# Hash attention and a gated feed-forward layer in one kernel: another order of the opening, and the second head pair hashed as one

## The chip, the core and the metric

The kernel runs on one core of a Trainium2 chip. The core has five engines that each work through their own list of instructions in order and wait for each other by semaphores: TensorE (PE; its weight loads are shown as PEld), VectorE (DVE), ScalarE (ACT), GpSimd (POOL) and SyncE (SP). [...] Loads and stores between memory and SBUF are DMAs, issued by SP and GpSimd (and one or two by ScalarE). The metric is device time in microseconds (us), the median of the runs.

## The reference

Inputs are q, k, v of shape (4, 8, 768, 64), that is 4 batches and 8 heads, a projection of 64 x 6, and the weights of a gated feed-forward layer (512 wide, 1536 inside).

```python
q_bits = (np.einsum('bhsd,dk->bhsk', q, proj) > 0)      # 6 bits a token, k the same
q_bucket = np.sum(q_bits * 2 ** np.arange(6), axis=-1)  # k_bucket the same
mask = q_bucket[:, :, :, None] == k_bucket[:, :, None, :]
scores = np.where(mask, (q @ k.T) / 8, -1e9)
attn = softmax(scores)                                  # + 1e-9 in the divisor
x = (attn @ v) as (4 * 768 tokens, 512)
xn = x / sqrt(mean(x * x) + 1e-6) * rms_g
out = (silu(xn @ w_gate) * (xn @ w_val)) @ w_out
```

A query sees only the keys whose six hash bits are the same as its own.

## The kernel before

**The mask as extra rows of a product.** Scores come from one product per 128 keys and 384 queries. Its operands lie in a buffer QK: rows 0 to 63 hold k or q in fp16, rows 64 to 75 twelve rows of hash bits (six bits and their complements, scaled by -32 and 16), so that a key and a query with different bits get a large negative score. A score product reads 76 rows (`KROWS`) or, for the pairs listed in `score_rows`, all 128; rows 76 to 127 must then be zero, which `clear_rows` writes. There are six QK buffers, `qkbuf`, taken in turn by (batch, head pair): pairs (0,0) to (0,3) get 0 to 3, (1,0) and (1,1) get 4 and 5, (1,2) gets 0 again.

**How k, q and bits get there.** A load brings raw rows. For batch 0 and the first two pairs of batch 1, `keep` turns a head's k or q on TensorE (three 128 x 128 products with the identity, tile t_ps) and copies it from PSUM to an fp32 tile (kT, qT); `cast_half` casts 64 rows at a time to fp16 into QK, on GpSimd, and for one half of q on ScalarE. `hash_bank` multiplies the fp32 tiles with the projection, four products into one PSUM bank (d_ps), `signs` compares on VectorE and writes the tile bits, and twelve-row pieces of it are moved into QK by VectorE, GpSimd or a DMA. `hash_head` hashes one head per bank, `hash_heads` the two heads of a pair in one bank. In the kernel before, heads 0 to 3 of batch 0 are hashed one by one and the later pairs as pairs.

**Windows, turns, slots.** The work is cut into 8 windows w of 384 queries (two for each batch). A turn (w, hp) is one head pair of one window. `TURNS` gives their order: (0,0), (1,0), (0,1), (0,2), (0,3), (1,1), (1,2), (1,3), and so on. Each turn has two heads, each head three slots p of two key blocks. Slot g is one `scores` (two products into one of two PSUM tiles s_ps) and one `probs` (exp on ScalarE, 128 x 768). After a head's three slots, `av` multiplies the probabilities with v into the bank o_ps, in two halves. There is one o_ps bank; a turn's two heads fill it. `attn_out` then empties it on VectorE: an add (otmp) and a reciprocal (rcp). `attn_x` makes x and its squares sq, on GpSimd for most turns (for turns (0,2) and (0,3) on VectorE), and `sumsq` sums the squares on VectorE (ssp). When all four pairs of a window are done, `norm`, `scale_x` and `turn_x` make the layer's input, and `gate`, `value` and `project` are the feed-forward products of that window, spread between the score products of later slots.

**The order is written out by hand.** A dictionary `plan` holds what is emitted at each step s; the last loop goes through the steps: `scores(s + 1)`, then work of rank below 3, then `probs(s + 1)`, then the rest by rank. The order of emission is the order on each engine; nothing reorders it afterwards. So an operation that waits holds up everything that was planned after it on its engine. Window 0's gate products begin at step 42.

Three places in the plan matter here. The x of turn (0,1) and its squares come at step 20 (`o_step`), the emptying of o_ps for turn (0,2) at step 26, and the first AV product of turn (0,3), head 6, at step 28. Turns (0,0) and (1,0) end at steps 8 and 14; before, their x and squares come at steps 8 and 17 (`o_step`, `o_last`). The sums of squares of the turns (0,0), (1,0) and (0,1) come at steps 12, 18 and 24. Twice, GpSimd also issues halves of the weights, at steps 2 and 6 and at steps 19 and 24.

```python
at(end - 1, av, w, h, 0, 9)
at(end, av, w, h, 9, 18)
...
at(end, o_step, w, h // 2, rank=4.5)      # add, reciprocal, x, squares
...
at(end + late, s_step, w, h // 2, rank=5)  # sum of squares
```

Of the kernel before, what the change touches and what calls it, by code (L numbers as in the profile page):

```python
# [8 lines left out]
FP32 = mybir.dt.float32  # L9
# [7 lines left out]
S = 768  # L17
D = 64
# [3 lines left out]
HALF = 384  # L22
KROWS = D + 12
# [25 lines left out]
def kernel(  # L49
# [12 lines left out]
    nc = tc.nc  # L62
    PSUM = bass.MemoryType.PSUM

    const = ctx.enter_context(tc.tile_pool(name="const", bufs=1))
# [17 lines left out]
    pk = const.tile([128, 48], FP32, name="pk")  # L83
    pq = const.tile([128, 48], FP32, name="pq")
    thr = const.tile([128, 1], FP32, name="thr")
    scl = const.tile([128, 1], FP32, name="scl")
    mhalf = const.tile([128, 3], FP32, name="mhalf")
    gcol = const.tile([128, 4], FP32, name="gcol")
# [46 lines left out]
        if (b, hp) not in QK:  # L135
            QK[b, hp] = qkbuf[len(QK) % len(qkbuf)]

    def clear_rows(i):
        nc.gpsimd.memset(qkbuf[i][D:128].rearrange("p h n -> p (h n)").bitcast(FP32), 0.0)

    def score_rows(b, hp):
        return slice(0, 128 if (b, hp) in ((1, 0), (1, 1)) or b > 1 else KROWS)

    def t_tile(b, hp, which):
        T0[b, hp, which] = tpool.tile(
# [3 lines left out]
    def t0(b, h, which):  # L149
        hp, hh = divmod(h, 2)  # L150
        return T0[b, hp, which][:, hh * HALF : (hh + 1) * HALF]
# [35 lines left out]
    def keep(eng, b, h, which, room=None):  # L187
        ps = turn_pe(b, h, which, room)
        (eng.copy if eng is nc.scalar else eng.tensor_copy)(t0(b, h, which), ps)
# [155 lines left out]
    def idle(ps, n):  # L345

        for _ in range(n):
            nc.tensor.matmul(ps, ones16, ones16, start=True, stop=True)  # L348

    def scores(g):  # L350
        w, h, p = SLOTS[g]
        ps = scps.tile([128, 2, 512], FP32, name="s_ps")
        idle(ps[:, 0, HALF:512], {0: 8, 3: 6}.get(g, 0))
        for j in range(2):
            nc.tensor.matmul(  # L355
                ps[:, j, 0:HALF], k_cols(w // 2, h, 2 * p + j), q_cols(w, h),
                start=True, stop=True,
            )
        sps[g] = ps
# [25 lines left out]
    def attn_out(w, hp):  # L385
        b = w // 2
        if w not in x:
            x[w] = xpool.tile([128, 3, DMODEL], FP32, name="x")
            ssp[w] = xpool.tile([128, 3, 4], FP32, name="ssp")
        o = ot.pop((w, hp))  # L390
        tmp = spool.tile([128, 3, 2, 66], FP32, name="otmp")
        nc.vector.tensor_add(  # L392
            tmp[:, :, :, 0:65], o[:, :, :, 0:65],
            cvb[b % 2][:, 2 * hp : 2 * hp + 2, 0:65].unsqueeze(1).to_broadcast([128, 3, 2, 65]),
        )
        r = spool.tile([128, 3, 2, 1], FP32, name="rcp")
        nc.vector.reciprocal(r, tmp[:, :, :, 64:65])  # L397
        return tmp, r

    def attn_x(w, hp, tmp, r):  # L400
        xd = x[w][:, :, 128 * hp : 128 * hp + 128]
        urgent = (w, hp) in ((0, 2), (0, 3))
        eng = nc.vector if urgent else nc.gpsimd
        eng.tensor_mul(  # L404
            xd.rearrange("p c (h d) -> p c h d", h=2), tmp[:, :, :, 0:64],
            r.to_broadcast([128, 3, 2, 64]),
        )
        sq = spool.tile([128, 3, 128], FP32, name="sq")
        if urgent:
            for c in range(3):  # L410
                nc.vector.scalar_tensor_tensor(
                    out=sq[:, c], in0=xd[:, c], scalar=1.0, in1=xd[:, c],
                    op0=ALU.mult, op1=ALU.mult, accum_out=ssp[w][:, c, hp : hp + 1],
                )
        else:
            nc.gpsimd.tensor_mul(sq, xd, xd)  # L416
        return sq
# [97 lines left out]
        load_rows(nc.sync, 0, hp, which)  # L515

    nc.vector.memset(ones16, 1.0)
    make_identity(nc, ident)
    nc.gpsimd.dma_start(out=pn[64:128], in_=proj)
    nc.vector.memset(pm, 0.0)  # L520
# [21 lines left out]
    for i in range(2):  # L542
        nc.gpsimd.memset(vls[i][:, :, :, 64:65], 1.0)
        nc.gpsimd.memset(vsum[i][:, :, 64:65], 6.0)
    clear_rows(4)
    clear_rows(5)

    def load_w(dst, src, n0, n1):
        nc.gpsimd.dma_start(
# [15 lines left out]
    def columns_of_proj():  # L565
        rows = pn.unsqueeze(1).to_broadcast([128, 4, 6])
        for t, sign in ((pk, 1.0), (pq, -1.0)):
            nc.vector.scalar_tensor_tensor(
                out=t[:, 0:24].rearrange("p (c n) -> p c n", n=6), in0=pm, scalar=sign,
                in1=rows, op0=ALU.mult, op1=ALU.mult,  # L570
            )
# [5 lines left out]
    def casts(b, hp, i):  # L577
        for par in range(2):
            if not i % 2 or par:
                cast_half(b, 2 * hp + i // 2, "kq"[i % 2], par)  # L580
# [2 lines left out]
    keep(nc.scalar, 0, 0, "q")  # L583
    cast_half(0, 0, "q", 0, nc.scalar)
    columns_of_proj()
    idle(wz[:, 0:128], 5)
    bits0 = hash_head(0)
    keep(nc.scalar, 0, 1, "k")
    bits0((nc.vector, nc.vector, nc.vector))
    keep(nc.scalar, 0, 1, "q", scps.tile([128, 2, 512], FP32, name="s_ps")[:, 0, 0:HALF])  # L590
    casts(0, 0, 0)
    casts(0, 0, 2)
    cast_half(0, 1, "q", 0)
    scores(0)
    bits1 = hash_head(1)
    scores(1)
    probs(0)
# [9 lines left out]
    def at(s, f, *a, rank=3):  # L607
        plan[s].append((rank, len(plan[s]), lambda: f(*a)))
# [3 lines left out]

    moves = {}

    def hash_one(h):
        moves[h] = hash_head(h)
        moves[h]((nc.sync,), 3)

    def hash_pair(b, hp):
        moves[b, hp] = hash_heads(b, hp)  # L620
        odd = [(0, 2), (1, 2), (0, 3), (1, 3)]
# [2 lines left out]

    for h in range(2):
        at(1 + h, cast_half, 0, h, "q", 1)
        at(h, (bits0, bits1)[h], (nc.vector,), 3)

    for hp, turns, sv in ((1, (1, 2, 3, 5), 8), (2, (7, 8, 9, 10), 17), (3, (12, 13, 14, 15), 22)):
        for i, s in enumerate(turns):  # L630
            at(s, keep_pair, 0, hp, i)
            at(s + 1, casts, 0, hp, i)
            if i % 2:
                at(s + 2, cast_half, 0, 2 * hp + i // 2, "q", 0, nc.scalar)
        at(sv, v_prep, 0, hp)

    for h, s in ((2, 4), (3, 7)):
        at(s, hash_one, h)
        for t in range(3):
            at(s + 1 + t, lambda h=h, t=t: moves[h]((nc.vector,), t), rank=5)  # L640
    for hp, s, slots in ((2, 12, (13, 14, 15, 16)), (3, 17, (18, 19, 20, 21))):
        at(s, hash_pair, 0, hp)
        for i, s in enumerate(slots):
            at(s, lambda hp=hp, i=i: moves[0, hp](nc.vector, [divmod(i, 2)]), rank=5)
# [8 lines left out]


    for hp, loads, turns, sh, evens, sv in (
        (0, (9, 11, 13), (20, 21, 24, 27), 33, (41, 42), (27, 44)),
        (1, (13, 14, 36), (29, 31, 33, 35), 40, (45, 47), (49, 51)),
    ):
        for which, sl in zip("kqv", loads):
            at(sl, load_rows, nc.sync, 1, hp, which)  # L660
        for i, sl in enumerate(turns):
            at(sl, keep_pair, 1, hp, i)
            at(sl + 1, casts, 1, hp, i)
        at(sh, hash_pair, 1, hp)
        for hh, sl in enumerate(evens):
            at(sl, cast_half, 1, 2 * hp + hh, "q", 0)
        at(sv[0], v_prep, 1, hp)
        at(sv[1], v_sum, 1, hp)
# [30 lines left out]
    for hp, s in enumerate((48, 62, 64, 78)):  # L699
        at(s, v_mean, 1, hp, 2)  # L700

    for i, s in ((2, 76), (3, 78), (0, 97), (1, 98)):
        at(s, clear_rows, i, rank=6)

    gts, sqs = {}, {}
# [20 lines left out]
    for w in range(8):  # L726
        for h in range(H):
            end = LAST[w, h] + (2 if (w, h) == (0, 7) else 3)
            at(end - 1, av, w, h, 0, 9)
            at(end, av, w, h, 9, 18)  # L730
            if h % 2:
                if (w, h) == (1, 1):
                    at(end, o_first, w, 0, rank=4.5)
                    at(end + 3, o_last, w, 0, rank=4.5)
                else:
                    at(end, o_step, w, h // 2, rank=4.5)
                if (w, h) not in ((0, 5), (0, 7)):
                    late = 3 if h == 7 and w < 7 else 4
                    at(end + late, s_step, w, h // 2, rank=5)
        s0 = 24 * w + 42  # L740
        n0 = {0: 11, 2: 7, 3: 13, 4: 13, 5: 13, 6: 13}.get(w, 11)
        at(s0 - n0, norm, w, rank=5)
        for c in range(3):
            scale, rank = {0: 6, 2: 6 - c}.get(w, 8 - c), 1
            turn = {0: (4, 3, 2), 2: (4, 2, 1)}.get(w, (5, 3, 1))[c]
            if w in BY_DMA and c < 2:
                scale, turn, rank = 11 - c, 11 - c, 6
            at(s0 - scale, scale_x, w, c, rank=5)
            at(s0 - turn, turn_x, w, c, rank=rank)
        seen = set()  # L750
        for ft in range(NF):
            for f, s in ((g_step, s0 + 16 * ft // NF), (v_step, s0 + (32 * ft + 16) // (2 * NF))):
                at(s, f, w, ft, rank=4 if s in seen else 2)
                seen.add(s)
        for i in range(9 if w < 7 else 6):
            c, j = divmod(i, 3)
            at(s0 + 16 + i, project, w, c, 4 * j, 4 * j + 4, rank=1 if i == 8 else 3)
# [55 lines left out]
```

## Time and profile before

| | |
|---|---|
| median of 3 runs | 329.44 us (329.18 to 329.79) |
| the profiled execution | 329.47 us, of which the span of its instructions is 327.6 us |
| busy share of the span | TensorE 98%, VectorE 72%, ScalarE 64%, GpSimd 50% |
| first score product | 8.37 us |
| score products of slots 19 and 20 | 28.04 us |
| x of turn (0,1) on GpSimd | 32.53 us |
| first gate product | 48.72 us |

A row of a timeline gives start, duration, engine, line, operation, output<-input with shapes, and how often it ran in a row (x3 with one duration is the three together); the square bracket at its end is the idle time of the engine before it and what ended that. The chain of waits follows the end of the execution back to the start: at each step to what released it. A product's busy time includes its passage through the array, so that products in a row overlap: 0.48 us is shown for two score products of which the next can start 0.33 us later. GpSimd's spans are rough.

### The profile page before, as it was taken

What the parts mean: (1) busy time and instruction counts of PE and PEld (TensorE: products, weight loads), DVE (VectorE), ACT (ScalarE), POOL (GpSimd) and SP (SyncE); (2) the same over time, 40 slices, a digit from 0 to 9 for tenths busy, and PEclk for the clock granted to TensorE, in tenths of its full rate; (3) what the DMA queues carried; (4) which work ended last, traced back from release to release, by engine and by line L of the source; (5) the groups of instructions that cost most, each with busy time, mean ns of one, the idle gap of its engine ahead of it and who ended that gap; (6) DMA issues with size and microseconds to landing.
All of it is one profiled execution on the core that took longest, in us unless ns stands there. A gap on an engine that the chain in (4) does not pass through costs nothing.

```text
span 327.6 us, 7853 instructions
## 1 busy us (share of the span) xinstructions
PE 321.5 (98%) x2975; PEld 199.5 (61%) x2975; DVE 234.9 (72%) x526; ACT 208.1 (64%) x324; POOL 165.4 (50%) x238
## 2 busy tenths in 40 slices
PE   8998999999999999999999999999999999999995
PEld 7576766655566556655566656566566656655654
DVE  4798896888598976989487865967267824793860
ACT  3788986775576666657576766667677766423331
POOL 7887977278658685686734274733221320230000
PEclk9999999999999999999999999999999999999999
DMA  7998988984359729911470814001200012002002
GB/s 216 358 212 244 165 131 154 151 179 70 119 109 172 128 48 226 155 39 26 130 128 18 150 24 152 3 18 22 78 32 2 11 24 98 0 3 96 2 0 97
DMA packets 85509, 32.69 MB, mean 100 GB/s; under 512 B 70376, under 2 KB 82400, under 8 KB 85472
## 3 DMA queue, kind: packets, MB, share of 16 engines
q1 hardware_dynamic: 81392, 27.28, 35.2%
q0 software_dynamic: 3712, 4.72, 9.3%
q8 instruction: 23, 0.38, 0.5%
q10 hardware_dynamic: 368, 0.20, 0.2%
q14 instruction: 14, 0.11, 0.1%
HBM read 28.58 MB, written 6.29 MB: 106 GB/s over the span
## 4 chain that ended last, share of the span: by engine, by line
PE 94%; DMA 2%; ACT 2%; DVE 0%; issue 0%; DVEq 0%; ACTq 0%
PE v_ps L483 19%; PE s_ps L355 19%; PE y_ps L496 18%; PE g_ps L473 15%; PE o_ps L377 10%; PE d_ps L221 4%; PE s_ps L473 4%; PE t_ps L181 2%; DMA QK<-bits 2%; ACT psb L365 1%; PE z_ps L348 1%; PE x_ps L458 1%; DMA out_dram<-ysb 1%; PE m_ps L336 1%; DVE bits L228 0%
## 5 line engine op out<-in xcount | busy, mean ns | idle before, releaser
L365 ACT ACTIVATE psb<-s_ps 128x768 f16<-128x768 f32 x192 | 150.7, 809 | 30.1 <-PE s_ps L355 28.1
L355 PE MATMUL s_ps<-QK 128*128 128x384 f16 (+1 forms) x384 | 93.7, 326 | 1.3 <-DMA QK<-bits 0.5
L483 PE MATMUL v_ps<-xnT,wv 128*128 128x384 f16 x384 | 78.1, 326 | 0.0
L496 PE MATMUL y_ps<-wo,ht 128*128 128x512 f16 x276 | 69.2, 379 | 0.0
L404 POOL TENSOR_TENSOR x<-otmp,rcp 128x384 f32<-128x384 f32 x30 | 25.7, 857 | 83.4 <-DVE rcp L397 83.2
L377 PEld LDWEIGHTS <-psb 128*128 128x128 f16 x1152 | 51.7, 98 | 21.8 <-issue 3.7
L475 ACT ACTIVATE t<-g_ps 128x384 f32<-128x384 f32 x78 | 38.2, 490 | 40.7 <-PE g_ps L473 38.2
L473 PE MATMUL g_ps<-xnT,wg 128*128 128x384 f16 x312 | 63.5, 326 | 0.0
L484 DVE SCALAR_TENSOR_TENSOR t<-t,g_ps 128x384 f32<-128x384 f32 x78 | 42.9, 550 | 28.3 <-ACT t L475 28.2
L485 DVE SCALAR_TENSOR_TENSOR ht<-t,v_ps 128x384 f16<-128x384 f32 x96 | 53.2, 554 | 11.5 <-PE v_ps L483 1.0
L377 PE MATMUL o_ps<-vl,psb 128*128 128x65 f16 x1152 | 56.0, 193 | 0.0
L483 PEld LDWEIGHTS <-wv 128*128 128x128 f16 x384 | 36.5, 98 | 22.9
L473 PEld LDWEIGHTS <-wg 128*128 128x128 f16 x384 | 36.1, 98 | 23.0
L496 PEld LDWEIGHTS <-ht 128*128 128x128 f16 x276 | 26.3, 98 | 26.5 <-issue 2.1
L355 PEld LDWEIGHTS <-QK 128*128 128x128 f16 (+1 forms) x384 | 31.1, 97 | 16.8 <-issue 3.1
L503 ACT COPY ysb<-y_ps 128x512 f32<-128x512 f32 x23 | 13.5, 585 | 24.3 <-PE y_ps L496 23.7
L392 DVE TENSOR_TENSOR otmp<-o_ps,cvb 128x390 f32<-128x390 f32 x32 | 17.9, 559 | 14.9 <-PE o_ps L377 14.8
L416 POOL TENSOR_TENSOR sq<-x 128x384 f32<-128x384 f32 x30 | 25.5, 849 | 2.4
L213 POOL CAST QK<-kT 64x768 f16<-64x768 f32 x20 | 17.0, 848 | 10.8 <-DVE kT L205 8.9
L213 POOL CAST QK<-qT 64x768 f16<-64x768 f32 x20 | 16.5, 823 | 10.8 <-DVE qT L205 8.1
L205 DVE STREAM_TRANSPOSE kT<-kL 128x192 f32<-128x192 f32 x40 | 19.7, 521 | 0.0
L205 DVE STREAM_TRANSPOSE qT<-qL 128x192 f32<-128x192 f32 x40 | 19.4, 518 | 0.0
(81 smaller groups left out, 307.2 us busy)
## 6 DMA issues: line engine op xcount, KB each, us to landing
vL<-in_v_dram SPq DMA_DIRECT2D x16, 384.0 KB
out_dram<-ysb SPq DMA_DIRECT2D x23, 256.0 KB
kL<-in_k_dram SPq DMA_DIRECT2D x40, 96.0 KB
qL<-in_q_dram SPq DMA_DIRECT2D x40, 96.0 KB
kL<-in_k_dram SPq DMA_DIRECT2D x5, 384.0 KB
qL<-in_q_dram SPq DMA_DIRECT2D x5, 384.0 KB
wg<-in_moe_w_gate_dram POOLq DMA_DIRECT2D x2, 768.0 KB, 8.5
wv<-in_moe_w_val_dram POOLq DMA_DIRECT2D x2, 768.0 KB, 9.6
```

The costliest lines, as they stand in the source:

```text
L205: nc.vector.transpose(dst.rearrange("p (c t r) -> p r c t", c=6, r=4)[:, r : r + 1], src.rearrange("p (r c) d -> p r c d", r=4)[:, r : r + 1],
L213: nc.gpsimd.tensor_copy(QK[b, hp][0:64, hh, o : o + S], T0[b, hp, which][64 * hh : 64 * hh + 64, :])
L355: nc.tensor.matmul(ps[:, j, 0:HALF], k_cols(w // 2, h, 2 * p + j), q_cols(w, h), start=True, stop=True,)
L365: nc.scalar.activation(psb[w, h][:, p], sps.pop(g)[:, :, 0:HALF], AF.Exp, scale=ESCALE,)
L377: nc.tensor.matmul(o[:, c, hh, 0:65], psb[w, h][:, jt // 2, jt % 2, 128 * c : 128 * c + 128], vls[b % 2][:, h, v_chunk(b, h, jt), 0:65], s ...
L404: eng.tensor_mul(xd.rearrange("p c (h d) -> p c h d", h=2), tmp[:, :, :, 0:64], r.to_broadcast([128, 3, 2, 64]),)
L473: nc.tensor.matmul(g, wg[:, kt, fs], xnT[w][:, kt], start=(kt == 0), stop=(kt == 3))
L475: nc.scalar.activation(t, g, AF.Tanh, scale=0.5)
L483: nc.tensor.matmul(vv, wv[:, kt, fs], xnT[w][:, kt], start=(kt == 0), stop=(kt == 3))
L484: nc.vector.scalar_tensor_tensor(out=t, in0=t, scalar=1.0, in1=g, op0=ALU.add, op1=ALU.mult)
L485: nc.vector.scalar_tensor_tensor(out=ht[w][:, ft], in0=t, scalar=0.5, in1=vv, op0=ALU.mult, op1=ALU.mult)
L496: nc.tensor.matmul(y, ht[w][:, ft, c * 128 : (c + 1) * 128], wo[:, ft, :], start=(ft == 0), stop=(ft == NF - 1),)
```

## The change

It does the following.

- The second pair, heads 2 and 3 of batch 0, is hashed in one bank by `hash_pair` at step 4 (`hash_one` for each, at steps 4 and 7, goes). Its bits come by four DMAs and four VectorE copies; pairs 2 and 3 are hashed at steps 11 and 16 instead of 12 and 17, with their copies shifted.
- Turns of pair 1 move to steps 1, 1, 1, 2, the first of them ahead of `scores(0)` with its copy after it; those of pairs 2 and 3 come one step earlier. Of 14 idle products (128 columns each, their result is not used) in front of scores 0 and 3, four stay, in front of score 0.
- Loads of k and q for pair (1,0) move from steps 9 and 11 to step 5. The fourth block of bits of heads 0 and 1 is copied at steps 2 and 4 instead of 0 and 1.
- Zeros: GpSimd clears buffers 1 and 2 at the start, ScalarE buffer 4 (a copy of a column of zeros), VectorE buffer 5 in two halves. Later GpSimd clears buffers 0 (step 50) and 3 (step 78) alone. All pairs but (0,0) and (0,3) then use 128 rows in their score products.
- x and squares of turns (0,0) and (1,0) move to steps 22 and 24. Their sums come at steps 24 and 26, that of turn (0,1) at step 22, all with rank 4. otmp and rcp get three buffers, sq one instead of two.

```diff
-    def clear_rows(i):
-        nc.gpsimd.memset(qkbuf[i][D:128].rearrange("p h n -> p (h n)").bitcast(FP32), 0.0)
+    def clear_rows(i, eng=nc.gpsimd, heads=(0, 1)):
...
     def score_rows(b, hp):
-        return slice(0, 128 if (b, hp) in ((1, 0), (1, 1)) or b > 1 else KROWS)
+        return slice(0, KROWS if (b, hp) in ((0, 0), (0, 3)) else 128)
...
-        idle(ps[:, 0, HALF:512], {0: 8, 3: 6}.get(g, 0))
+        idle(ps[:, 0, HALF:512], {0: 4}.get(g, 0))
...
-        tmp = spool.tile([128, 3, 2, 66], FP32, name="otmp")
+        tmp = spool.tile([128, 3, 2, 66], FP32, name="otmp", bufs=3)
...
-        r = spool.tile([128, 3, 2, 1], FP32, name="rcp")
+        r = spool.tile([128, 3, 2, 1], FP32, name="rcp", bufs=3)
...
-        sq = spool.tile([128, 3, 128], FP32, name="sq")
+        sq = spool.tile([128, 3, 128], FP32, name="sq", bufs=1)
...
-    clear_rows(4)
-    clear_rows(5)
+    clear_rows(1)
+    clear_rows(2)
+    clear_rows(4, nc.scalar)
+    clear_rows(5, nc.vector, (0,))
...
     columns_of_proj()
+    clear_rows(5, nc.vector, (1,))
     idle(wz[:, 0:128], 5)
...
+    next_k = turn_pe(0, 2, "k")
     casts(0, 0, 0)
     casts(0, 0, 2)
     cast_half(0, 1, "q", 0)
     scores(0)
+    nc.vector.tensor_copy(t0(0, 2, "k"), next_k)
     bits1 = hash_head(1)
...
-        at(h, (bits0, bits1)[h], (nc.vector,), 3)
-
-    for hp, turns, sv in ((1, (1, 2, 3, 5), 8), (2, (7, 8, 9, 10), 17), (3, (12, 13, 14, 15), 22)):
+        at(2 + 2 * h, (bits0, bits1)[h], (nc.vector,), 3, rank=6)
+
+    for hp, turns, sv in ((1, (1, 1, 1, 2), 8), (2, (6, 7, 8, 9), 17), (3, (11, 12, 13, 14), 22)):
         for i, s in enumerate(turns):
-            at(s, keep_pair, 0, hp, i)
+            if hp > 1 or i > 0:
+                at(s, keep_pair, 0, hp, i)
...
-    for h, s in ((2, 4), (3, 7)):
-        at(s, hash_one, h)
-        for t in range(3):
-            at(s + 1 + t, lambda h=h, t=t: moves[h]((nc.vector,), t), rank=5)
-    for hp, s, slots in ((2, 12, (13, 14, 15, 16)), (3, 17, (18, 19, 20, 21))):
+    for hp, s, slots in (
+        (1, 4, (5, 6, 8, 9)), (2, 11, (12, 12, 14, 15)), (3, 16, (17, 18, 19, 20))
+    ):
         at(s, hash_pair, 0, hp)
...
-        (0, (9, 11, 13), (20, 21, 24, 27), 33, (41, 42), (27, 44)),
+        (0, (5, 5, 13), (20, 21, 24, 27), 33, (41, 42), (27, 44)),
...
-    for i, s in ((2, 76), (3, 78), (0, 97), (1, 98)):
+    for i, s in ((0, 50), (3, 78)):
         at(s, clear_rows, i, rank=6)
...
-                if (w, h) == (1, 1):
+                if w < 2 and h == 1:
                     at(end, o_first, w, 0, rank=4.5)
-                    at(end + 3, o_last, w, 0, rank=4.5)
+                    at(22 + 2 * w, o_last, w, 0, rank=4.5)
+                    at(24 + 2 * w, s_step, w, 0, rank=4)
                 else:
                     at(end, o_step, w, h // 2, rank=4.5)
-                if (w, h) not in ((0, 5), (0, 7)):
+                if (w, h) not in ((0, 1), (0, 5), (0, 7), (1, 1)):
                     late = 3 if h == 7 and w < 7 else 4
-                    at(end + late, s_step, w, h // 2, rank=5)
+                    if (w, h) == (0, 3):
+                        at(22, s_step, w, 1, rank=4)
+                    else:
+                        at(end + late, s_step, w, h // 2, rank=5)
```

More of the change, by code (lines that the diff above doesn't have):

```diff
@@ L85 @@
     thr = const.tile([128, 1], FP32, name="thr")
+    zcol = const.tile([128, 1], FP32, name="zcol")
     scl = const.tile([128, 1], FP32, name="scl")
@@ L136, in qk_tile @@
             QK[b, hp] = qkbuf[len(QK) % len(qkbuf)]
-    def clear_rows(i):
-        nc.gpsimd.memset(qkbuf[i][D:128].rearrange("p h n -> p (h n)").bitcast(FP32), 0.0)
+    def clear_rows(i, eng=nc.gpsimd, heads=(0, 1)):
+        for h in (heads if eng is nc.vector else (0,)):
+            part = qkbuf[i][D:128, h] if eng is nc.vector else (
+                qkbuf[i][D:128].rearrange("p h n -> p (h n)"))
+            part = part.bitcast(FP32)
+            if eng is nc.scalar:
+                eng.copy(part, zcol[D:128].to_broadcast([D, 2 * S]))
+            else:
+                eng.memset(part, 0.0)
     def score_rows(b, hp):
-        return slice(0, 128 if (b, hp) in ((1, 0), (1, 1)) or b > 1 else KROWS)
+        return slice(0, KROWS if (b, hp) in ((0, 0), (0, 3)) else 128)
     def t_tile(b, hp, which):
@@ L517 @@
     nc.vector.memset(ones16, 1.0)
+    nc.vector.memset(zcol, 0.0)
     make_identity(nc, ident)
@@ L613 @@
     moves = {}
-    def hash_one(h):
-        moves[h] = hash_head(h)
-        moves[h]((nc.sync,), 3)
     def hash_pair(b, hp):
@@ L731 @@
             if h % 2:
-                if (w, h) == (1, 1):
+                if w < 2 and h == 1:
                     at(end, o_first, w, 0, rank=4.5)
-                    at(end + 3, o_last, w, 0, rank=4.5)
+                    at(22 + 2 * w, o_last, w, 0, rank=4.5)
+                    at(24 + 2 * w, s_step, w, 0, rank=4)
                 else:
                     at(end, o_step, w, h // 2, rank=4.5)
-                if (w, h) not in ((0, 5), (0, 7)):
+                if (w, h) not in ((0, 1), (0, 5), (0, 7), (1, 1)):
                     late = 3 if h == 7 and w < 7 else 4
-                    at(end + late, s_step, w, h // 2, rank=5)
+                    if (w, h) == (0, 3):
+                        at(22, s_step, w, 1, rank=4)
+                    else:
+                        at(end + late, s_step, w, h // 2, rank=5)
         s0 = 24 * w + 42
```

## The prediction

> **What bounds the kernel now.** First the page: the span, and the chain that ended last.
>
> ```profile
> span 327.6 us, 7853 instructions
> ...
> PE 94%; DMA 2%; ACT 2%; DVE 0%; issue 0%; DVEq 0%; ACTq 0%
> ```
>
> TensorE is 94% of the chain, so work moved on the other engines wins only where TensorE waits for it now, and loses where TensorE would wait afterwards. Second, the chain of waits over the first 50 us, where nearly all edits lie. Columns: start, length, what.
>
> ```profile
> 1.05 3.17 PE z_ps L348 x28
> 4.22 1.28 PE t_ps L181 x6
> ...
> 5.98 0.94 PE d_ps L221 x8
> ...
> 10.97 0.50 PE s_ps L348 x6
> ...
> 11.79 0.33 PE t_ps L181 x3
> ...
> 16.81 0.78 PE d_ps L221 x8
> ...
> 23.48 5.21 DMA QK<-bits
> ```
>
> The one long foreign piece is a copy of hash bits by DMA, issued at 23.48 and landed at 28.69, for pair 2. What TensorE itself stood still for stands in the view of who waited for whom, up to 50 us (total, times, longest):
>
> ```profile
> PE s_ps L355 <- DMA QK<-bits: 0.5, 1, 0.5
> PE s_ps L355 <- ACT psb L365: 0.3, 1, 0.3
> ```
>
> So that stall costs TensorE 0.5 us, and 0.3 more for the exp it held up. Third, the timelines by engine behind it: GpSimd, then VectorE, then TensorE.
>
> ```profile
> 32.53 0.89 POOL L404 TENSOR_TENSOR x<-otmp,rcp 128x384 f32<-128x384 f32 x1 [1.60 <-DVE rcp L397]
> 33.50 0.82 POOL L416 TENSOR_TENSOR sq<-x 128x384 f32<-128x384 f32 x1
> 34.27 1.05 POOL L197 CAST QK<-kT 64x384 f16<-64x384 f32 x2
> 35.39 0.82 POOL L321 CAST vl<-vL 128x768 f16<-128x768 f32 x1
> 36.28 0.50 POOL L197 CAST QK<-qT 64x384 f16<-64x384 f32 x1
> 36.73 0.80 POOL L549 DMA_DIRECT2D wv<-in_moe_w_val_dram  x1
> 37.58 0.52 POOL L197 CAST QK<-kT 64x384 f16<-64x384 f32 x1
> ```
> ```profile
> 34.63 0.55 DVE L420 TENSOR_REDUCE ssp<-sq 128x3 f32<-128x384 f32 x1
> 35.53 0.56 DVE L392 TENSOR_TENSOR otmp<-o_ps,cvb 128x390 f32<-128x390 f32 x1 [0.35 <-PE o_ps L377]
> ...
> 40.15 0.55 DVE L392 TENSOR_TENSOR otmp<-o_ps,cvb 128x390 f32<-128x390 f32 x1
> ```
> ```profile
> 36.50 0.44 PE L377 MATMUL o_ps<-vl,psb 128*128 128x65 f16 x9
> ```
>
> GpSimd works without a pause from 32.53 (x of turn (0,1), step 20) to 37.58: x, square, two casts, v, a cast, the issue of wv. The vector add at 35.53 (step 26, turn (0,2)) empties the only output bank; it waits for nothing but TensorE. The AV product at 36.50 (step 28) is the first that needs the bank empty again. Most of the price comes from these rows.
>
> **The second pair hashed as one.** One bank of fp32 products goes, 0.78 (16.81) to 0.94 (5.98), taken as 0.9 of TensorE. VectorE loses one sign operation and two bit copies. SP gets four bit DMAs for two, and right behind them, at step 5 instead of 9 and 11, the loads of k and q of (1,0). GpSimd comes to the weights wg and wv behind two casts and one cast more (0.5 each); nothing needs those weights before step 42.
>
> **Fewer idle products.** The six before score 3 took 0.50 in the chain, some of it a wait for ACT's exp anyway; taken as 0.4. The four dropped before score 0 stand beside an ACT copy that score 0 waits out: nothing, and 0.4 at most were the copy earlier.
>
> **Transposes earlier.** Sixteen stay sixteen. Three now stand in front of score 0 (0.33, row 11.79) and need pair 1's k, whose landing no row shows. Score 0 comes 0 to 0.8 later, by nothing or by the stall of 0.5 and the products; I take 0.4, near the 0.33 that certainly stands in the way.
>
> **Zeros first.** GpSimd clears two buffers at the start as before, and two instead of four later, beside other work: nothing. The other two buffers are cleared in pauses:
>
> ```profile
> L139 POOL MEMSET QK<- 64x1536 f32 x2 | 2.7, 1372 | 0.1
> ```
> ```profile
> 4.90 0.56 DVE L189 COPY kT<-t_ps 128x384 f32<-128x384 f32 x1 [1.40 <-PE t_ps L181]
> ...
> 6.98 0.68 DVE L228 TENSOR_SCALAR bits<-d_ps,thr,scl 128x384 f16<-128x384 f32 x1 [1.34 <-PE d_ps L221]
> ```
> ```profile
> 5.54 0.48 ACT L189 COPY qT<-t_ps 128x384 f32<-128x384 f32 x1 [2.94 <-PE t_ps L181]
> ```
>
> GpSimd's 1.37 for a buffer makes 0.69 for a half (estimate for VectorE), inside pauses of 1.40 and 1.34. ACT's clear has four times the columns of the copy at 5.54, so at most 4 x 0.48 = 1.9 of its 2.94. Without that cover the second half would put its 0.69 in front of the first hash. Scores over 128 rows in place of 76 stream the same columns: nothing.
>
> **Bits and loads in another order.** For pair 2 the DMA is issued about 1.5 us earlier (one step of 0.9, and the bank that is gone), and so are the loads in front of it. If it takes 5.21 again, the stall of 0.8 goes. If the total of bytes sets the landing, it stays at 28.69 and eats what was won before. So the gain g at step 20 lies between 0 and 0.9 + 0.4 - 0.4 + 0.8 = 1.7. I take 0.9, the middle, since both ends rest on the same row.
>
> **x and squares later.** Here the order of instructions on two engines decides. GpSimd has, from step 20 on: x and square (0,1), two casts, v, a cast, x and square (0,0), wv, x and square (1,0). VectorE has: sum (0,1), a copy, sum (0,0), sum (1,0), and only then the add of (0,2). Each sum waits for GpSimd's square. So the add stands behind the whole of GpSimd's list, and behind the add stand all later vector work and step 28's AV product, which TensorE cannot pass. The price:
>
> - x (0,1) starts at 32.53 - g.
> - The list takes 37.58 - 32.53 = 5.05 and two more pairs of x and square at 34.27 - 32.53 = 1.74: 8.5. The last square ends at 41.0 - g.
> - Sum 0.55, add 0.56, hand-overs 0.2: step 28's product starts at 42.3 - g instead of 36.50, so 5.8 - g later: 4.9 with g = 0.9, ends 4.1 and 5.8.
> - TensorE comes to that product about g earlier than before, so it stands idle for 5.8 us in one piece.
>
> **The clock behind that pause.** Two windows at the end of the span (stretch, length, busy PE, PEld, DVE, ACT, POOL, granted clock, DMA):
>
> ```profile
> 324.00:326.00 2.00, 0.06 (x2) 0.00 (x0) 0.29 (x1) 0.00 (x0) 0.00 (x0) 1.00 0.43 131
> 326.00:327.62 1.62, 0.00 (x0) 0.00 (x0) 0.00 (x0) 0.00 (x0) 0.00 (x0) 0.70 0.02 5
> ```
>
> TensorE is done at 324.06, and a mean of 0.70 over the last 1.62 us is half speed from 326.65: 2.6 idle us halved the clock. At the start, six transposes took 1.28 (0.213 each) at 4.22, three took 0.33 (0.11) at 11.79, and the bank at 5.98 still took 0.94. So products ran at half pace from 1.05 to between 5.5 and 6.9, 4.4 to 5.9 us, in which 2.2 to 2.9 were lost. Behind a pause of 5.8 us I expect the same again. Part is hidden: from add to add (35.53 to 40.15) VectorE has its own list, about 1.0 longer than TensorE's products in that stretch. I take 1.6; ends 0 and 2.9. [...]
>
> **The rest.** Three buffers for otmp and rcp keep two late ones alive: nothing. One buffer for sq makes square (0,0) wait for sum (0,1), which is done a good three us before. Behind step 28 the order is the old one and TensorE leads the chain, so what is late stays late.
>
> **Sum.** The profiled execution took 329.47 (its span 327.6 and 1.9 around it), beside a median of 329.44. 329.47 + 4.9 + 1.6 = 336.0. Ends: 329.47 + 4.1 = 333.6 and 329.47 + 5.8 + 2.9 = 338.2. Up to 0.8, the size of the waits seen above, could be won back by TensorE after the pause: 332.8.
>
> **Rivals.**
>
> - The pause comes, but the clock stays. For it: no idle stretch inside the span shows a fall, only the one at its end. Against: 5.8 is over twice 2.6. Time 329.47 + 4.9 = 334.4.
> - Faster: the add of (0,2) isn't held up, and the bank and the bits are won. It decides if GpSimd's list is through 1.2 us (sum, add) before TensorE gets to step 28: in 36.5 - 1.2 - 32.5 = 2.8 us instead of 8.5. Against: the durations above, and that its pause of 1.60 lies in front of the list, which starts with a wait for step 20's reciprocal. Time 329.47 less 0.9 to 1.7: 328.2.
> - The bits land as late as now: g = 0, so 329.47 + 5.8 + 1.6 = 336.9, up to 338.2. For it: 5.21 us for 9 KB is queueing. [...]
>
> **How the numbers follow.** Forecast 0.58 (336.0, its own range 334.8 to 337.2), clock stays 0.20, bits as late 0.10, faster 0.09, loss and gain cancel 0.03. The range 332.8 to 338.2 leaves out the last two and little else. What a measurement of this kernel can tell from no change is 0.2%, 0.66 us: faster 0.09, same 0.03, slower 0.88.
>
> **What would show it.** In the profile after: TensorE idle for 5 to 6 us in one piece between 34 and 43 us, ahead of an o_ps product; VectorE's sums waiting some 2 us, twice, for GpSimd's sq; a granted clock below 1.00 in the windows there; one hash bank fewer; less waiting for the bits. I am wrong if that pause is under 2 us, if the clock stays at 1.00, or if the time lost is won back before 50 us.

## The result, and the profile after

The changed kernel takes 339.5 us (median of 6 runs, 337.64 to 340.62), the one before 329.43 beside it: ratio 1.0296, 95% interval 1.0266 to 1.0326, some 10 us slower. The profiled execution took 339.77 with a span of 337.6. Three lines of its page: the span, the granted clock in 40 slices, and the engines' shares of the chain that ended last.

```profile
span 337.6 us, 7820 instructions
...
PEclk9998979999999999999999999999999999999999
...
PE 88%; DMA 5%; POOL 2%; ACT 2%; DVE 1%; issue 1%; SPq 0%; DVEq 0%; POOLq 0%; ACTq 0%
```

A slice is 8.4 us, and a 9 means 0.9 or more: the clock fell in the fourth slice (8, from 25 to 34 us) and the sixth (7, from 42 to 51 us). TensorE has 88% of the chain instead of 94%; DMA has 5% for 2%, and POOL, which wasn't there, 2%. TensorE's waits up to 66 us (total, times, longest), in the view of who waited for whom:

```profile
PE s_ps L363 <- DMA QK<-bits: 6.0, 2, 3.6
PE o_ps L385 <- DVE otmp L400: 2.6, 1, 2.6
PE t_ps L189 <- DMA kL<-in_k_dram: 1.9, 1, 1.9
```

The first row stands for two waits, 3.6 for pair 2's bits and 2.35 for pair 3's. The kernel before has 0.5 for the bits and none of the others. The chain of waits over the same stretch (start, length, what) puts them in a row:

```profile
2.60 6.63 DMA kL<-in_k_dram
...
22.80 8.83 DMA QK<-bits
...
35.92 0.90 POOL x L412
...
44.99 0.56 DVE otmp L400
```

Pair 1's k lands at 9.23 and score 0 waits for it. Pair 2's bits are issued at 22.80, 0.7 earlier than before, and land at 31.63, 2.9 later. Then x of turn (0,1) starts at 35.92, and the predicted list runs from there to the add at 44.99 and step 28's AV product at 45.60. VectorE's timeline shows the hold-up inside that list, the sums waiting for GpSimd's squares and the add of (0,2) behind them:

```profile
42.02 0.56 DVE L428 TENSOR_REDUCE ssp<-sq 128x3 f32<-128x384 f32 x1 [0.87 <-POOL sq L424]
44.52 0.56 DVE L428 TENSOR_REDUCE ssp<-sq 128x3 f32<-128x384 f32 x1 [1.95 <-POOL sq L424]
44.99 0.55 DVE L400 TENSOR_TENSOR otmp<-o_ps,cvb 128x390 f32<-128x390 f32 x1
```

TensorE's timeline: score 0, the score products of slot 16, the wait for pair 3's bits, step 28's AV, and the first transpose of the layer's input (x_ps), which is as far as the opening reaches. Below it two of these rows of the kernel before.

```profile
9.94 0.49 PE L363 MATMUL s_ps<-QK 76*128 76x384 f16 x2
...
24.77 1.00 PE L363 MATMUL s_ps<-QK 128*128 128x384 f16 x4
...
39.88 0.34 PE L363 MATMUL s_ps<-QK 76*128 76x384 f16 x1 [2.35 <-DMA QK<-bits]
...
45.60 0.68 PE L385 MATMUL o_ps<-vl,psb 128*128 128x65 f16 x9 [2.56 <-DVE otmp L400]
...
55.57 0.39 PE L466 MATMUL x_ps<-ident,xn 128*128 128x128 f16 x4
```

```profile
24.54 0.49 PE L355 MATMUL s_ps<-QK 76*128 76x384 f16 x2
...
36.50 0.44 PE L377 MATMUL o_ps<-vl,psb 128*128 128x65 f16 x9
```

Before, x_ps began at 44.96; the opening is 10.61 longer. From x_ps to the end it is 284.51 before (329.47 - 44.96) and 284.20 after, so the loss lies in the opening. Behind the 2.35 us of waiting for pair 3's bits the clock stays at 1.00, from 36 to 45 us. The windows (busy PE, PEld, DVE, ACT, POOL, then the granted clock) show it halved behind the other two, for pair 2's bits (3.6) and for the add (2.6); in windows of 1 us it is 0.50 from 32 to 35 and from 46 to 49 us:

```profile
28.00:32.00 4.00, 0.37 (x3) 0.21 (x3) 1.42 (x5) 0.52 (x1) 0.33 (x1) 1.00 1.10 315
32.00:36.00 4.00, 4.00 (x34) 3.08 (x32) 1.45 (x4) 2.80 (x4) 0.08 (x1) 0.58 1.13 252
...
44.00:48.00 4.00, 2.40 (x24) 2.08 (x25) 3.37 (x12) 0.81 (x1) 2.26 (x4) 0.70 1.12 185
```

### The profile page after: what moved, and what is told of

Same layout as the page of the kernel before. It is cut to its first block, busy times and chain, and to the rows that moved or that the text cites. A ratio compares the mean times of both kernels' runs of the same rounds, so it can differ in the third digit from the quotient of the medians.

```text
span 337.6 us, 7820 instructions
## 1 busy us (share of the span) xinstructions
PE 322.3 (95%) x2957; PEld 200.1 (59%) x2957; DVE 235.0 (70%) x526; ACT 209.6 (62%) x325; POOL 162.3 (48%) x236
## 4 chain that ended last, share of the span: by engine, by line
PE 88%; DMA 5%; POOL 2%; ACT 2%; DVE 1%; issue 1%; SPq 0%; DVEq 0%; POOLq 0%; ACTq 0%
PE v_ps L491 18%; PE y_ps L504 18%; PE s_ps L363 17%; PE g_ps L481 15%; PE o_ps L385 10%; PE s_ps L481 3%; PE d_ps L229 3%; DMA QK<-bits 3%; DMA kL<-in_k_dram 2%; ACT psb L373 1%; PE t_ps L189 1%; PE x_ps L466 1%; POOL x L412 1%; POOL sq L424 1%; DMA out_dram<-ysb 1%
## 5 line engine op out<-in xcount | busy, mean ns | idle before, releaser
L363 PE MATMUL s_ps<-QK 128*128 128x384 f16 (+1 forms) x384 | 95.3, 330 | 6.4 <-DMA QK<-bits 6.0
L385 PEld LDWEIGHTS <-psb 128*128 128x128 f16 x1152 | 52.7, 99 | 24.7 <-issue 3.5
L385 PE MATMUL o_ps<-vl,psb 128*128 128x65 f16 x1152 | 57.0, 195 | 2.6 <-DVE otmp L400 2.6
L221 POOL CAST QK<-kT 64x768 f16<-64x768 f32 x20 | 16.8, 841 | 12.1 <-DVE kT L213 9.2
L221 POOL CAST QK<-qT 64x768 f16<-64x768 f32 x20 | 16.5, 823 | 12.1 <-DVE qT L213 9.4
```

Source lines behind the costliest of these rows:

```text
L221: nc.gpsimd.tensor_copy(QK[b, hp][0:64, hh, o : o + S], T0[b, hp, which][64 * hh : 64 * hh + 64, :])
L363: nc.tensor.matmul(ps[:, j, 0:HALF], k_cols(w // 2, h, 2 * p + j), q_cols(w, h), start=True, stop=True,)
L385: nc.tensor.matmul(o[:, c, hh, 0:65], psb[w, h][:, jt // 2, jt % 2, 128 * c : 128 * c + 128], vls[b % 2][:, h, v_chunk(b, h, jt), 0:65], s ...
```

## The experiments

The question is what the 10 us are made of: x and squares late, as predicted, or the bits, and if these, why they land late although they are issued earlier. Medians are given with the lowest and highest run; the kernel before, on the same chip, had 329.42 to 329.53.

**1. x and squares late, alone, on the kernel before.**

```diff
-                if (w, h) == (1, 1):
+                if w < 2 and h == 1:
                     at(end, o_first, w, 0, rank=4.5)
-                    at(end + 3, o_last, w, 0, rank=4.5)
+                    at(22 + 2 * w, o_last, w, 0, rank=4.5)
+                    at(24 + 2 * w, s_step, w, 0, rank=4)
...
+                    if (w, h) == (0, 3):
+                        at(22, s_step, w, 1, rank=4)
```

> The kernel before, with x, squares and sums of turns (0,0), (0,1), (1,0) moved to steps 22 to 26 as in the changed kernel (one buffer for sq, three for otmp and rcp); nothing else changed. Theory, by the terms of the prediction: GpSimd's list of 8.5 us in front of the add of (0,2), TensorE idle about 5.8 us in one piece ahead of step 28's AV, the clock halved behind it: 329.4 + 5.8 + 1.6 = 336.8, and 335.2 if the clock stays. Rival (TensorE has other work, the list costs little by itself): under 332.

337.14 (337.07 to 338.46), ratio 1.024 (1.0212 to 1.0268). TensorE's timeline:

```profile
42.15 0.68 PE L377 MATMUL o_ps<-vl,psb 128*128 128x65 f16 x9 [1.02 <-DVE otmp L392]
...
52.08 0.39 PE L458 MATMUL x_ps<-ident,xn 128*128 128x128 f16 x4
```

Step 28's AV starts 5.65 later than before (36.50), and from there to x_ps it takes 9.93 instead of 8.46: 1.5 for the clock. Both terms are the predicted ones (5.8 and 1.6). Only the shape was missed: TensorE isn't idle for 5.8 in one piece. It waits 1.0 there; the rest of the time had gone by in an earlier wait for pair 3's bits (2.3) and in work at half speed (0.50 in every window from 36 to 45 us).

**2. The same, with the pauses filled.**

```diff
-        idle(ps[:, 0, HALF:512], {0: 8, 3: 6}.get(g, 0))
+        idle(ps[:, 0, HALF:512], {0: 8, 3: 6, 25: 40, 29: 60}.get(g, 0))
```

> The kernel before with x and squares late, 337.1, and in addition 40 idle products of 128 columns ahead of score 25 and 60 ahead of score 29, so that TensorE is busy in the two pauses in front of step 28's AV. Theory (the clock's share is 1.6 as in the prediction): the granted clock stays above 0.9 from 35 to 46 us, step 28's AV starts near 42.1 as without them, since GpSimd's list sets it, and from there to the first transpose of xn it takes 8.5 us in place of 10.0: 335.6. Rival (the clock costs nothing here, TensorE's own work is not what the rest waits for): 337 or more.

335.57 (334.96 to 336.29). The window from 36 to 40 us, whose clock was 0.50 in experiment 1, and TensorE's timeline:

```profile
36.00:40.00 4.00, 4.00 (x63) 3.44 (x61) 1.11 (x2) 2.80 (x4) 3.74 (x5) 1.00 0.88 132
```

```profile
42.00 0.45 PE L377 MATMUL o_ps<-vl,psb 128*128 128x65 f16 x9
...
50.37 0.39 PE L458 MATMUL x_ps<-ident,xn 128*128 128x128 f16 x4
```

The AV starts where it did, since GpSimd's list sets it, and x_ps follows 8.37 later. The difference of the medians, 1.57 of 337.14, is the clock's share of x and squares; from the AV to x_ps it is 1.56 (9.93 - 8.37).

**3. The changed kernel with x and squares back.** The same lines the other way round, and the buffers of otmp, rcp and sq as before.

> The changed kernel, with x, squares and sums of turns (0,0), (0,1) and (1,0) back where they stood before, and the buffers of otmp, rcp and sq too. Theory (two causes in a row, bits first, x and squares second): the pause of 2.6 us in front of step 28 goes and the second fall of the clock with it, the 6.0 us of waits for bits stay: 335.5 to 337. Rival (x and squares are the main cause, as the prediction had it, 5.8 and 1.6): 331 to 333.

331.4 (330.12 to 331.88), ratio 1.0044 (1.0028 to 1.0061). The rival holds: x and squares are worth 8.1 of the 10 here. My theory of that moment, which put the bits first, falls. What is left, 2.0, goes with a wait for pair 2's bits (experiment 7 takes it away):

```profile
PE s_ps L363 <- DMA QK<-bits: 3.0, 1, 3.0
```

```profile
21.01 8.76 DMA QK<-bits
```

Issued 2.5 earlier than before, they land at 29.77, 1.1 later.

**4. The changed kernel with the weights' first halves issued earlier.**

```diff
-        at(2 + 4 * i, load_w, t, src, 0, 768)
+        at(1 + 2 * i, load_w, t, src, 0, 768, rank=0)
```

> The changed kernel, with the first halves of wg and wv issued on GpSimd two or three casts earlier, about where they stood before (14 and 17 us in place of 17.28 and 18.53); all else as changed. Theory (the late weights leave the DMA engines idle at 17 to 20 us, so weights and the bits of pair 2 share them later): the bits of pair 2 land near 29 in place of 31.63, TensorE's 6.0 us of waits for bits fall to about 3, the x of turn (0,1) starts near 33 in place of 35.92 and step 28's AV with it; the pause in front of step 28 grows from 2.6 towards 5, being no longer hidden. Time 336.0 to 337.5. Rival (the bits are late because the loads of (1,0) and the four copies of pair 1 stand in front of them, the weights don't matter): landing 31 to 32 again, 339 to 340.

336.41 (334.97 to 336.7). The time is the expected one, the way is not. wg is issued at 12.1, and no wait for pair 2's bits is left. Now it is pair 1's bits that come late, as TensorE's timeline shows, and pair 3's (1.95):

```profile
23.04 0.32 PE L363 MATMUL s_ps<-QK 128*128 128x384 f16 x1 [1.77 <-DMA QK<-bits]
...
41.95 0.67 PE L385 MATMUL o_ps<-vl,psb 128*128 128x65 f16 x9 [2.21 <-DVE otmp L400]
```

So the bytes of the weights seem to hold up whichever bits come next in time. x of (0,1) starts at 32.26 and step 28's AV again 9.7 later.

**5. The kernel before with the weights' first halves issued later.**

```diff
-        at(2 + 4 * i, load_w, t, src, 0, 768)
+        at(4 + i, load_w, t, src, 0, 768)
```

> The kernel before, with the first halves of wg and wv issued on GpSimd some casts later, at about 17 and 18 us in place of 14.11 and 16.95; nothing else changed. Theory (late weights alone make the bits late): the bits of pair 2 land near 31 in place of 28.69, TensorE waits 2 to 3 us for them in place of 0.5, the clock falls behind it: 331.5 to 334. Rival (the weights don't matter): within 0.7 of the kernel before, 329.4.

330.5 (329.54 to 333.81), ratio 1.0047 (1.0017 to 1.0077): between the two expectations. The profiled execution is the slowest of ten. GpSimd's issue of wg (14.11 before), the chain's row of the bits, TensorE's wait, and two windows:

```profile
16.21 0.81 POOL L549 DMA_DIRECT2D wg<-in_moe_w_gate_dram  x1
```

```profile
24.05 6.33 DMA QK<-bits
```

```profile
30.52 1.12 PE L355 MATMUL s_ps<-QK 76*128 76x384 f16 x3 [1.58 <-DMA QK<-bits]
```

```profile
31.00:32.00 1.00, 1.00 (x12) 0.72 (x11) 0.60 (x2) 0.97 (x2) 0.50 (x1) 0.50 0.96 334
...
37.00:38.00 1.00, 1.00 (x14) 0.76 (x13) 0.00 (x0) 0.44 (x1) 0.88 (x3) 0.91 1.29 205
```

With wg 2.1 later the bits land at 30.38, 1.7 later. Of that 0.6 is their own later issue (24.05 for 23.48), for the opening as a whole runs 0.6 later in this execution. So some 1.1 is left for the weights, which I had costed at nothing: they do move the bits. What that costs goes with the clock: the two executions at 333.8 have a mean granted clock of 0.987 and 0.988, the seven up to 330.71 have 0.998 to 1.00.

**6. The weights' first halves in two parts each, on experiment 3.**

```diff
-        at(2 + 4 * i, load_w, t, src, 0, 768)
+        at(2 + 4 * i, load_w, t, src, 0, 384)
+        at(12 + i, load_w, t, src, 384, 768, rank=5)
```

> The changed kernel with x and squares back, and in addition the first halves of wg and wv cut in two: one quarter each where the halves were issued, the other quarters only behind the issue of pair 2's bits (GpSimd's steps 12 and 13). Theory (pair 2's bits land when the bytes of the weights in front of them are through, 14.2 to 15.0 us behind the issue of wg in every profile so far, whenever they are issued themselves): with half the bytes they land by 26, TensorE's wait of 3.0 us and the fall of the clock behind it go: 327.3 to 328.8. Rival (the bits are late by the four copies of pair 1 and the loads of (1,0) in their own queue): they land near 29.8 again, 331 to 332.

332.74 (329.54 to 333.76): the time is a miss, the bits aren't. There is no wait for pair 2's bits. The DMA queues from 23 to 24 us (q0 GpSimd's, q1 SP's; packets, MB, share), experiment 3 first:

```profile
q0 software_dynamic: 83, 0.13, 70.1%
q1 hardware_dynamic: 82, 0.13, 40.3%
```

```profile
q1 hardware_dynamic: 259, 0.37, 101.0%
q0 software_dynamic: 10, 0.01, 4.5%
```

In experiment 3, where both queues have work, that microsecond has 83 packets of GpSimd's and 82 of SP's, and SP's loads move 0.13 MB; in this one, with 10 packets of GpSimd's, they move 0.37. So k and q of (1,0), 0.79 MB that stand in front of the bits in SP's own queue, move at about a third of their speed while weights run; that the bits do stand behind q, experiment 7 shows. The time was lost elsewhere: the two more issues cost GpSimd 0.80 and 0.74, its square of (1,0) comes late, and VectorE's sum waits for it with TensorE's bank behind:

```profile
30.98 0.55 DVE L428 TENSOR_REDUCE ssp<-sq 128x3 f32<-128x384 f32 x1 [2.50 <-POOL sq L424]
```

```profile
33.04 0.43 PE L385 MATMUL o_ps<-vl,psb 128*128 128x65 f16 x9 [2.19 <-DVE otmp L400]
```

It is the hold-up of x and squares once more, from another cause.

**7. The loads of (1,0) back, on experiment 3.** SP has issued pair 1's four copies until about 18, so k goes out at the same time as in experiment 3 (18.01 for 17.86). What changes is q, which now comes behind pair 2's bits.

```diff
-        (0, (5, 5, 13), (20, 21, 24, 27), 33, (41, 42), (27, 44)),
+        (0, (9, 11, 13), (20, 21, 24, 27), 33, (41, 42), (27, 44)),
```

> The changed kernel with x and squares back, and in addition the loads of k and q of (1,0) back at steps 9 and 11. Theory (bytes of the weights): these loads stand in front of pair 2's bits either way; the landing stays near 29.8 and the time within 0.7 of 331.4. Rival (the loads issued earlier hold up the bits): landing by 28.7, 329.3 to 330.5.

329.09 (327.86 to 329.73), ratio 0.9982 (0.9965 to 0.9998). The rival holds. TensorE's timeline:

```profile
27.85 0.66 PE L363 MATMUL s_ps<-QK 128*128 128x384 f16 x3 [0.70 <-DMA QK<-bits]
...
33.23 0.34 PE L363 MATMUL s_ps<-QK 76*128 76x384 f16 x1 [0.61 <-DMA QK<-bits]
```

The wait for pair 2's bits ends at 27.85, 1.9 earlier than they landed in experiment 3, and falls from 3.0 to 0.7. So the bits did wait for q of (1,0) in front of them. But that alone isn't what the change added: in the kernel before q stands in front of pair 2's bits too (issued at 19.82, the bits at 23.48). What differs is what moves beside it. By the DMA queues, k and q move there from 23 to 28 us with 0.30 MB of weights beside them; in experiment 3, where wg is issued at 15.48 instead of 14.11, from 22 to 28 us with 0.73 MB; in the changed kernel (17.28) from 24 to 30 us with 0.74 MB. Taking q away cures the wait. That the later weights caused it fits these rows and experiments 4 and 5, but no run moves the weights back on experiment 3.

**8. The loads of (1,0) back, on the changed kernel.** The same line, x and squares late.

> The changed kernel with the loads of k and q of (1,0) back at steps 9 and 11, which puts q behind pair 2's bits in SP's queue; x and squares late as changed. Theory (two causes that add: the load of q in front of the bits, and x and squares): the bits of pair 2 land in time, TensorE waits under 1 us for them, step 28 waits for the add of (0,2) with what is left of the 5.8, and the clock falls once: 329.1 (the kernel that has x and squares back too) + 7.4 (the prediction's terms for x and squares) = 336.5, 335.8 to 337.4. Rival (x and squares decide alone when step 28 starts, so that the bits in front of it don't matter): 338.5 to 340, as the changed kernel.

334.61 (333.92 to 335.31), below either expectation. The bits of pair 2 are in time, and x of (0,1) starts at 31.19. Another wait takes most of the hold-up in step 28. GpSimd's timeline of this kernel, of experiment 7, and TensorE's of this one:

```profile
26.01 0.74 POOL L560 DMA_DIRECT2D wg<-in_moe_w_gate_dram  x1
31.19 0.89 POOL L412 TENSOR_TENSOR x<-otmp,rcp 128x384 f32<-128x384 f32 x1 [4.44 <-DVE rcp L405]
```

```profile
29.28 0.80 POOL L560 DMA_DIRECT2D wg<-in_moe_w_gate_dram  x1
```

```profile
36.38 0.50 PE L363 MATMUL s_ps<-QK 76*128 76x384 f16 x1 [4.13 <-DMA QK<-bits]
...
49.73 0.39 PE L466 MATMUL x_ps<-ident,xn 128*128 128x128 f16 x4
```

With x and squares gone from its list around 20 to 29 us, GpSimd issues the second half of wg 3.3 earlier, and pair 3's bits take 8.55 instead of 5.11. Experiment 1 has the same two things together: that issue at 27.96 instead of 30.13, and the wait of 2.3 for pair 3's bits. That the one causes the other is read from the profiles; no run separates it. The pause came early enough that the clock was back before step 28: from x to x_ps it is 18.54, 0.4 more than 9.68 and 8.46.

**9. The changed kernel once more.**

> The changed kernel once more, unchanged. If the late landing of pair 1's k (9.23 us in the changed kernel's profile, 7.3 with x and squares back, although the program is the same up to there) was a chance of that execution, it lands near 7.5 here, GpSimd issues wg near 15.5 in place of 17.28, and pair 2's bits land near 30 in place of 31.63. If the change causes it, all three come again. Time 338 to 340.5 either way, since step 28 waits for x and squares, whatever comes first.

338.84 (two runs). TensorE, GpSimd, and the chain's row of the bits:

```profile
8.16 0.49 PE L363 MATMUL s_ps<-QK 76*128 76x384 f16 x2
...
22.98 1.00 PE L363 MATMUL s_ps<-QK 128*128 128x384 f16 x4
...
43.85 0.68 PE L385 MATMUL o_ps<-vl,psb 128*128 128x65 f16 x9 [3.69 <-DVE otmp L400]
...
54.58 0.39 PE L466 MATMUL x_ps<-ident,xn 128*128 128x128 f16 x4
```

```profile
15.49 0.81 POOL L560 DMA_DIRECT2D wg<-in_moe_w_gate_dram  x1
...
34.17 0.89 POOL L412 TENSOR_TENSOR x<-otmp,rcp 128x384 f32<-128x384 f32 x1 [7.61 <-DVE rcp L405]
```

```profile
21.01 8.62 DMA QK<-bits
```

Score 0 starts at 8.16, not 9.94: the late k of the first profile was a chance of that execution. wg and the bits' landing (29.63) follow it. The waits for pair 2's bits (3.4) and for the add (3.7) come again, the one for k doesn't, and the one for pair 3's bits is 0.3.

**10. q of (1,1) behind pair 3's bits, on experiment 7.**

```diff
-        (1, (13, 14, 36), (29, 31, 33, 35), 40, (45, 47), (49, 51)),
+        (1, (13, 17, 36), (29, 31, 33, 35), 40, (45, 47), (49, 51)),
```

> The kernel with x, squares and the loads of (1,0) back (329.09), and in addition the load of q of (1,1) at step 17 in place of 14, behind pair 3's bits. Theory (bits stand behind the loads ahead of them in SP's own queue, 0.39 MB each): pair 3's bits land 1 to 1.5 us earlier, TensorE's 1.3 us of waits for bits fall under 0.5: 328.0 to 328.7. Rival (GpSimd's second half of wg sets the landing): 328.8 to 329.4.

328.51 (327.67 to 329.45), ratio 0.9978 (0.9961 to 0.9994): in the theory's range, and 0.2% faster than the kernel before. Of 1.3 us of waits for bits 0.3 is left. The gain over experiment 7, 0.6, isn't clear of noise, as the runs of the two overlap; the shorter waits are read from one profile each.

**11. Pair 1's first turn back behind score 0, on experiment 10.** `next_k` and its copy go, and `keep_pair(0, 1, 0)` is at step 1 again.

> As the kernel before in this call, and pair 1's first turn back at step 1, behind score 0. Theory (score 0 doesn't wait for the landing of pair 1's k any more): 0 to 0.4 faster than that one, 327.7 to 328.6. Rival (score 0 waits for ACT's copies as it did before the change, and the three transposes cost their 0.33 elsewhere): no difference, within 0.3.

329.88 (328.13 to 330.67): slower than experiment 10 where no loss was expected. Score 0 starts at 8.54, as it waits 0.4 for ScalarE's copy of q, so nothing is won. In the profiled execution, the slowest of ten, the load of q of (1,1), issued at 31.81, is what comes late:

```profile
40.77 0.52 PE L189 MATMUL t_ps<-ident,qL 128*128 128x128 f32 x3 [1.89 <-DMA qL<-in_q_dram]
```

So moving a load behind bits can move it too far.

**12. q of (1,0) behind pair 2's bits, alone, on the kernel before.**

```diff
-        (0, (9, 11, 13), (20, 21, 24, 27), 33, (41, 42), (27, 44)),
+        (0, (9, 12, 13), (20, 21, 24, 27), 33, (41, 42), (27, 44)),
```

> The kernel before with the load of q of (1,0) at step 12 in place of 11, which puts it behind pair 2's bits in SP's queue; nothing else changed. Theory (the bits stand behind SP's own loads): pair 2's bits land 1 to 1.5 us earlier than 28.69, TensorE's wait of 0.5 goes, pair 3's bits have a load more in front of them: 328.6 to 329.4. Rival (the weights on GpSimd's queue set the landing): 28.7 again and 329.4.

331.45 (330.41 to 334.19), ratio 1.0073 (1.0044 to 1.0103): slower, a miss. The profiled execution is the fastest of ten. Its slot 20 starts at 27.93 instead of 28.99, so pair 2's bits did land earlier. But a load more stands in front of pair 3's, and the only wait for bits, 0.8, is now there. The move pays only with pair 3's bits relieved too, as in experiment 10. The other executions took up to 4 us more than the profiled one, and the clock goes with it: the six up to 331.47 have a mean of 0.999 or 1.00, the four from 332.2 on 0.989 to 0.995. Which wait lets it fall there stays open.

## Why the prediction was wrong

The terms as this case's profiles measure them (us; "step 28" is its first AV product):

| kernel | x of (0,1) | step 28 | between | x_ps | between | profiled time |
|---|---|---|---|---|---|---|
| before | 32.53 | 36.50 | 3.97 | 44.96 | 8.46 | 329.47 |
| changed | 35.92 | 45.60 | 9.68 | 55.57 | 9.97 | 339.77 |
| changed, once more | 34.17 | 43.85 | 9.68 | 54.58 | 10.73 | 338.77 |
| 1, x late on before | 32.47 | 42.15 | 9.68 | 52.08 | 9.93 | 337.07 |
| 2, pauses filled | 32.31 | 42.00 | 9.69 | 50.37 | 8.37 | 335.25 |
| 4, weights earlier | 32.26 | 41.95 | 9.69 | 52.53 | 10.58 | 336.70 |

- **x and squares later: right.** The list takes 9.68 from x of (0,1) to step 28, in five profiles, against 9.77 in the prediction. Alone it costs 337.14 (experiment 1) against 336.8 by its terms. The pause of 5.8 in one piece did not come: 2.6 stands in front of step 28 in the changed kernel, 3.7 once more, 1.0 in experiment 1, since earlier waits and work at half speed use up the rest.
- **The clock: right.** 1.5 in the changed kernel (9.97 - 8.46), 2.3 once more, 2.1 in experiment 4, 1.57 by experiment 2; 1.6 predicted, with ends 0 and 2.9. It fell twice, though, and not behind one pause of 5.8; what the first fall costs is in the next point. The 1.6 was an estimate from the slow start of the span, and half pace there is read from durations: the granted clock of the kernel before shows 1.00 in every window from 1 to 8 us.
- **Bits and loads in another order: wrong, and this step decides.** It put the gain g at step 20 at 0.9, between 0 and 1.7. Measured is -3.39 (35.92 against 32.53), and -1.64 once more; the difference is the late k (below). From slot 16 to x of (0,1) it takes 11.15 (24.77 to 35.92) where it took 7.99 before (24.54 to 32.53): 3.2 lost, and the same 3.2 once more (22.98 to 34.17). I had held that the bits could at worst land at 28.69 again. That floor had no reason: the bits stand behind the loads of k and q (experiment 7), these move slower beside the weights (0.13 MB in a microsecond against 0.37, experiment 6), and the weights were moved in the same change. Experiment 7 takes q from in front of the bits, and 2.3 us of the median go; experiments 4 and 5 show that the time of the weights alone moves the bits. Since q stood in front before the change as well, the later weights are the likelier part of what the change added; how much of the 3.2 is theirs stays open.
- **GpSimd's weights behind three casts: wrong at "nothing needs those weights before step 42".** No product needs them earlier, but the bits come late while they are loaded beside k and q (experiments 4 and 5).
- **Transposes earlier: 0.4 taken, range 0 to 0.8.** 1.57 in the first profile (9.94 against 8.37), -0.2 once more. It exposes score 0 to the landing of pair 1's k, which varies between executions (9.23 in the first profile, 7.30 in experiment 3, whose program is the same up to there).
- **Hash bank and idle products: right.** From score 0 to slot 16 it took 16.17 and now takes 14.83; 1.34 won, 0.9 + 0.4 predicted.
- **Nothing behind step 28: right.** 284.20 from x_ps on, against 284.51. Nor do the 128 rows cost anything: in the kernel before a score product over 76 rows takes 0.325 on average, one over 128 rows 0.326.

So 336.0 becomes 339.8 by these rows: + 4.3 for g (0.9 to -3.39), - 0.1 for the list, - 0.1 for the clock, - 0.3 behind x_ps. Of the 4.3, 3.2 is the bits and 1.2 the late k (1.57 instead of 0.4). Once more, without the late k, it becomes 338.8: + 2.5 for g, + 0.7 for the clock, - 0.4 for the rest. Of the rivals, "the bits land as late as now" was nearest, and stopped one step short: they land later. The pieces don't add up by themselves: x and squares cost 8.1 with the bits late (experiment 3) and 5.5 with them in time (7 against 8), since TensorE's waits hide in each other and the clock falls once or twice, as the profiles suggest.

## What to carry to other kernels

When work is moved later on an engine that works in order, write down everything that stands behind it up to the first instruction that TensorE needs; that sum held to a tenth of a microsecond. A transfer's landing wants the same list, in its own queue and by bytes, with what shares the engines beside it; a small copy behind two loads is a large one (9 KB a copy behind 0.79 MB landed 8.83 us after the issue in the changed kernel), and "as late as now" is no worst case when what is loaded in front of it or beside it moves too. Work taken out of a list pulls up what follows it, and if that is a DMA, look at the next small transfer (experiments 1 and 8; read from profiles, not tested alone).

## What the runs showed of the hardware that was not expected

A short wait can halve the clock, and doesn't always. In experiment 5 TensorE stood 1.58 us, and the clock was at 0.50 in every window from 31 to 37 us. In experiment 11 it stood 1.89 us, and every window from 36 to 46 us shows 1.00, the one behind the wait among them:

```profile
41.00:42.00 1.00, 1.00 (x16) 0.68 (x14) 0.61 (x2) 0.02 (x1) 0.00 (x0) 1.00 1.22 176
```

In the changed kernel a wait of 2.35 us left the clock at 1.00 too. Nor need the fall come within the wait: in experiment 3 TensorE worked again from 29.82, and the clock fell at about 31.3: its mean from 30 to 35 us is 0.66, and three transposes at 31.40 took 0.85 where three at 36.15 took 0.49.

Experiments 5, 6 and 12 scatter by about 4 us between executions, where the kernel before scatters by 1.6. The mean granted clock of an execution goes with its time: in experiment 5 it is 0.998 to 1.00 up to 330.71 and 0.987 and 0.988 at 333.8; in experiment 6 it is 1.00 at 329.54, 0.994 or 0.995 from 331.45 to 332.83, and 0.989 or 0.990 above. So most of this scatter goes with whether the clock falls. Not all scatter does: in experiment 11 the executions from 328.13 to 330.67 all have 0.998 or 1.00.
